# A gated mix of linear attention and a SwiGLU block: the order and the queues of the first loads, and the place of one group of gate matmuls

## The chip, the cores and the metric

The kernel runs on one core of a Trainium2 chip. The core has five engines with an instruction stream each: TensorE (PE, matrix multiply; PEld is its weight load), VectorE (DVE), ScalarE (ACT), GpSimd (POOL) and SyncE (SP). DMA transfers are issued by an engine's queue, here by SP and ScalarE, and are carried out by 16 DMA engines that all queues share. The metric is device time in microseconds (us) of one execution, as a median over runs; less is better.

## The reference, cut to what matters

`x` is 2048 tokens of 512 numbers in bf16. One weight per column gives each token a gate `g`; the result mixes a linear-attention block (32 heads of 16) and a SwiGLU block (hidden width 1376).

```python
g = sigmoid((x * gate_w).sum(-1, keepdims=True))
# a: linear attention
q, k, v = split(x @ wqkv)                  # 32 heads, 16 wide
phi = lambda t: where(t > 0, t + 1, exp(t)) + 1e-6
kv  = einsum("bhsd,bhse->bhde", phi(k), v) # a sum over all tokens
z   = einsum("bhsd->bhd", phi(k))
o   = einsum("bhqd,bhde->bhqe", phi(q), kv) / (einsum("bhqd,bhd->bhq", phi(q), z) + 1e-6)
a   = o @ wo
# b: SwiGLU
b   = (silu(x @ w1) * (x @ w3)) @ w2
out = g * a + (1 - g) * b
```

## The kernel before

The tokens are cut into 16 tiles of 128 (numbered 0 to 15) and 4 blocks of 4 tiles (0 to 3). A matmul contracts over the 128 partitions, so the 512 columns of `x` are 4 chunks (`KC`). `x` is needed in two layouts: as it lies in memory (`x_sb`) and transposed (`xT`, columns on the partitions). The transposed one comes from DMA loads that transpose on the way, except for tile 0, which TensorE transposes itself (`emit_xT`, lines 180 to 192: four transposes, one copy by VectorE, one by ScalarE, line 192).

All loads are issued at the start. SP's queue issues, in this order: tile 0 of `x` (line 83), the transposing load of tile 1 and one of tiles 2 and 3 together (lines 88 and 89), then for blocks 1, 2 and 3 a transposing load (line 92) and a plain load of some tiles of `x` (line 97), and then the weights: wq, the last 96 columns of w1 and w3, the gate weights (line 102: one two-byte number per partition and chunk), wv, w1, w3, wo, w2. ScalarE's queue issues only the k weights `wk` in two halves (lines 84 and 85), ahead of a small exponential that loads its table.

TensorE's order is written out by hand (`manual_schedule`); that of the other engines is the framework's, which also places all semaphores and waits. TensorE's stages are:

1. warm-up matmuls on constants (`emit_warm`, lines 163 to 176): five groups of four matmuls with 32 weight columns each, and one of 128 columns; the transposes of tile 0; three more warm-up matmuls (line 417);
2. the k matmuls of tiles 0 to 3 (lines 418 to 421; line 195), 4 for each tile, in the order of the tiles. Each tile's result goes through `phi`: an exponential on ScalarE (line 145), two instructions on VectorE (lines 147 and 150), and a sum on GpSimd;
3. the k matmuls of tiles 4 to 15, mixed with `x`-transposed times phi(k) (`XP`, line 215), which sums over all tokens;
4. the q matmuls of block 0 and the remainder columns with the gate column (`r_ps`, line 251), then `kv` (64 matmuls of 32 columns, line 467), whose product with a mask on VectorE (line 471) feeds the `W` matmuls (line 487). Between these stand the 16 matmuls of the first w1 chunk (`emit_gate_tiled`, lines 326 to 333), in groups of four, one group per chunk of the contraction;
5. the SwiGLU matmuls (lines 345 and 353) and the output matmuls (lines 386 to 395) of all blocks.

The loads have no inputs that the program makes, so the engine that issues them waits only where the framework has it wait; an engine's instructions go out in order, a DMA issue among them.

Of the kernel before, what the change touches and what calls it, by code (L numbers as in the profile page):

```python
# [11 lines left out]
ENG = mybir.EngineType  # L12
# [5 lines left out]
def kernel(  # L18
# [12 lines left out]
    nc = tc.nc  # L31
    P = nc.NUM_PARTITIONS
# [5 lines left out]
    KC = D // P  # L38
    NT = S // P
    TB = 512  # L40
# [3 lines left out]
    FR = F - FC * P  # L44
    FM = FC * P
    NR = 2 * FR + 1
# [5 lines left out]
    x2d = A_x.flatten_outer_dims()  # L52
# [13 lines left out]
    xT = consts.tile([P, KC, S], BF16, name="xT")  # L66
# [5 lines left out]
    wr_sb = consts.tile([P, KC, 2 * P], BF16, name="wr_sb")  # L72
# [7 lines left out]
    x_r = x2d.rearrange("(t p) d -> p t d", p=P)  # L80
    dq = nc.sync
    TF = 1
    dq.dma_start(out=x_sb[:, 0, :], in_=x2d[0:P, :])
    nc.scalar.dma_start(out=wk_sb[:, 0:2, :], in_=wqkv_r[:, 0:2, D : 2 * D])  # L84
    nc.scalar.dma_start(out=wk_sb[:, 2:4, :], in_=wqkv_r[:, 2:4, D : 2 * D])
    pre = consts.tile([1, 1], FP32, name="pre")
    nc.scalar.activation(out=pre[:], in_=nc.const_aps.tensor(0.0, [1, 1], FP32), func=ACT.Exp)
    for tsl in (slice(P, 2 * P), slice(2 * P, TB)):
        dq.dma_start(out=xT[:, :, tsl], in_=x2d[tsl, :], transpose=True)
    x_cut = [TF, TPB + 2, 3 * TPB, NT]  # L90
    for tb in range(1, NTB):
        dq.dma_start(
            out=xT[:, :, tb * TB : (tb + 1) * TB], in_=x2d[tb * TB : (tb + 1) * TB, :],
            transpose=True,
# [3 lines left out]
    dq.dma_start(out=wq_sb[:], in_=wqkv_r[:, :, 0:D])  # L98
    dq.dma_start(out=wr_sb[:, :, 0:FR], in_=w1_r[:, :, FM:F])
    dq.dma_start(out=wr_sb[:, :, FR : 2 * FR], in_=w3_r[:, :, FM:F])  # L100
    with nc.allow_non_contiguous_dma(reason="one gate weight per partition and chunk"):
        dq.dma_start(
            out=wr_sb[:, :, 2 * FR : NR], in_=gate_w.rearrange("(kc d o) -> d kc o", d=P, o=1)
        )
    dq.dma_start(out=wv_sb[:], in_=wqkv_r[:, :, 2 * D : 3 * D])
    dq.dma_start(out=w1_sb[:], in_=w1_r[:, :, 0:FM])
    for fsl in (slice(0, FM // 2), slice(FM // 2, FM)):
# [12 lines left out]
        out=bm, in_=bm, pattern=[[-Dh, HPC], [0, Dh]], compare_op=ALU.is_ge, fill=0.0,  # L120
# [3 lines left out]
        out=bm, in_=bm, pattern=[[Dh, HPC], [0, Dh]], compare_op=ALU.is_ge, fill=0.0,  # L124
# [38 lines left out]
    def emit_warm(tiled, whole, tag="XP3"):  # L163
        warm = psX.tile([P, TB], FP32, tag=tag, name="warm")
        for n in tiled:
            for i in range(NG):
                gsl = slice(i * G, (i + 1) * G)
                nc.tensor.matmul(
                    warm[gsl, 0:n], lhsT=warm_l[:, gsl], rhs=warm_r[:, 0:n], start=True, stop=True
                )  # L170
        for n in whole:
            nc.tensor.matmul(
                warm[:, 0:n], lhsT=warm_l, rhs=warm_r[:, 0:n], start=True, stop=True
            )

    emit_warm((TB, TB, TB, TB, TB), (P,))

    st = {}

    def emit_xT(t):  # L180
        for h in range(2):
            xTp = psX.tile([P, 2, P], BF16, tag=f"XP{(2 * t + h) % 4}", name="xTp")
            for j in range(2):
                kc = 2 * h + j
                nc.tensor.transpose(
                    out=xTp[:, j, :], in_=x_sb[:, t, kc * P : (kc + 1) * P], identity=ident[:]
                )
            xT_t = xT[:, 2 * h : 2 * h + 2, t * P : (t + 1) * P]
            if h == 0:
                nc.vector.tensor_copy(out=xT_t, in_=xTp[:])  # L190
            else:
                nc.scalar.activation(out=xT_t, in_=xTp[:], func=ACT.Copy)
# [27 lines left out]
    def emit_q(tb, tt, pool, tag):  # L220
        t = tb * TPB + tt
        ts_tok = slice(t * P, (t + 1) * P)
        if tt == 0:
            st[tb, "pq"] = blk.tile([P, TPB, D], BF16, tag="pq", name="pq")
            st[tb, "den"] = blk.tile([P, TPB, H], FP32, tag="den", name="den")
        q_ps = pool.tile([P, D], FP32, tag=tag, name="q_ps")
        for kc in range(KC):
            nc.tensor.matmul(  # L228
                q_ps[:], lhsT=xT[:, kc, ts_tok], rhs=wq_sb[:, kc, :],
                start=(kc == 0), stop=(kc == KC - 1),  # L230
            )
        phi(st[tb, "pq"][:, tt, :], q_ps[:])
# [54 lines left out]
    def emit_omg(tb):  # L287
        om = work.tile([P, TPB], FP32, tag="om", name="om")
        nc.vector.tensor_scalar(
            out=om[:], in0=st[tb, "el"][:], scalar1=2.0, scalar2=2.0, op0=ALU.mult,  # L290
            op1=ALU.add,
        )
        nc.vector.reciprocal(out=omg[:, tb * TPB : (tb + 1) * TPB], in_=om[:])
# [29 lines left out]
            )  # L323
        st[tb, "pqT"] = pqT

    def emit_gate_tiled(gate_ps):
        for kc in range(KC):
            for i in range(NG):
                gsl = slice(i * G, (i + 1) * G)
                nc.tensor.matmul(  # L330
                    gate_ps[gsl, :], lhsT=w1_sb[:, kc, gsl], rhs=xT[:, kc, 0:TB],
                    start=(kc == 0), stop=(kc == KC - 1),
                )
# [79 lines left out]


    k0 = [psM.tile([P, D], FP32, tag="mm", name=f"k0_{t}") for t in range(TPB)]
    emit_xT(0)
    emit_warm((), (P, P, P))
    for t in range(TPB):
        for kc in range(KC):
# [14 lines left out]
    with tc.manual_schedule(engines={ENG.DVE}):  # L434
        Q = 32
        NB = D // Q
        zt = consts.tile([P, NB, Q], FP32, name="zt")
        nc.vector.transpose(out=zt[:].rearrange("p b f -> p (b f)"), in_=pks[:])
        w = Q // 2
        while w >= 1:  # L440
            nc.gpsimd.tensor_add(zt[:, :, 0:w], zt[:, :, 0:w], zt[:, :, w : 2 * w])
            w //= 2
        zq = zt[:, :, 0]
        z_up = consts.tile([P // 2, NB], FP32, name="z_up")
        z_h = consts.tile([P // 2, NB], FP32, name="z_h")
        z_hi = consts.tile([Q, NB], FP32, name="z_hi")
        z_col = consts.tile([P, NB], FP32, name="z_col")
        nc.gpsimd.tensor_copy(z_up[:], zq[P // 2 : P, :])
        nc.gpsimd.tensor_add(z_h[:], zq[0 : P // 2, :], z_up[:])
        nc.gpsimd.tensor_copy(z_hi[:], z_h[Q : 2 * Q, :])  # L450
        for b in range(P // Q):
            nc.gpsimd.tensor_add(z_col[b * Q : (b + 1) * Q, :], z_h[0:Q, :], z_hi[:])
        for dc in range(KC):
            if dc % 2 == 0:
                nc.scalar.activation(out=XP_sb[:, dc, :], in_=XP_ps[dc][:], func=ACT.Copy)
            else:
                nc.vector.tensor_copy(out=XP_sb[:, dc, :], in_=XP_ps[dc][:])

        emit_q(0, TPB - 1, psM, "mm")
        rem0 = [emit_rem_mm(0, half, psM, "mm") for half in range(2)]  # L460
        kvT_ps = psX.tile([P, KC, G], FP32, tag="XP0", name="kvT_ps")
        gate0 = psM.tile([P, TB], FP32, tag="mm", name="gate0")
        for c in range(KC):
            for dc in range(KC):
                for i in range(NG):
                    bsl = slice(c * P + i * G, c * P + (i + 1) * G)
                    nc.tensor.matmul(  # L467
                        kvT_ps[i * G : (i + 1) * G, c, :], lhsT=wv_sb[:, dc, bsl],
                        rhs=XP_sb[:, dc, bsl], start=(dc == 0), stop=(dc == KC - 1),
                    )  # L470
        nc.vector.tensor_tensor(
            out=kvT_sb[:], in0=kvT_ps[:],
            in1=diagmask[:, None, :].to_broadcast([P, KC, G]), op=ALU.mult,
        )
        for half in range(2):
            emit_rem_h(0, half, *rem0[half])
        nc.vector.transpose(
            out=z_sb[:].rearrange("p (b f) -> p b f", f=Q),
            in_=z_col[:, :, None].to_broadcast([P, NB, Q]),
        )  # L480

        emit_gate_tiled(gate0)
        W_ps = [psX.tile([P, D], FP32, tag=f"XP{i}", name=f"W_ps{i}") for i in range(NG)]
        for i in range(NG):
            gsl = slice(i * G, (i + 1) * G)
            for c in range(KC):
                nc.tensor.matmul(  # L487
                    W_ps[i][c * G : (c + 1) * G, :], lhsT=kvT_sb[gsl, c, :],
                    rhs=wo_sb[gsl, c, :], start=True, stop=True,
                )  # L490

        emit_omg(0)
        emit_ffn(0, 0, gate=gate0)
# [72 lines left out]
```

## Time and profile before

| | us |
|---|---|
| median of 3 runs (178.19 to 178.46) | 178.42 |
| the profiled execution | 178.12 |
| its span, first to last instruction | 176.3 |
| TensorE matmuls busy | 172.7 |
| VectorE busy | 119.9 |
| GpSimd busy | 66.9 |
| ScalarE busy | 64.5 |

The profile is one execution. Its lines give start and length in us, the engine, the line of the kernel, the operation, output and inputs, the number of instructions merged and, in brackets, the idle time of the engine before them with what ended it. Of the DMA engines' work, the plain picture is a full load in the first third of the span and little after it:

```
DMA  5999999911002311124000101240002022300002
GB/s 174 236 271 281 262 386 363 348 45 26 9 4 60 67 37 37 37 63 89 0 0 7 58 20 47 59 82 0 6 7 67 7 66 54 66 4 0 30 30 60
```

Each digit is the busy share, in tenths, of a fortieth of the span.

### The profile page before, as it was taken

What the parts mean: (1) busy time and instruction counts of PE and PEld (TensorE: products, weight loads), DVE (VectorE), ACT (ScalarE), POOL (GpSimd) and SP (SyncE); (2) the same over time, 40 slices, a digit from 0 to 9 for tenths busy, and PEclk for the clock granted to TensorE, in tenths of its full rate; (3) what the DMA queues carried; (4) which work ended last, traced back from release to release, by engine and by line L of the source; (5) the groups of instructions that cost most, each with busy time, mean ns of one, the idle gap of its engine ahead of it and who ended that gap; (6) DMA issues with size and microseconds to landing.
All of it is one profiled execution on the core that took longest, in us unless ns stands there. A gap on an engine that the chain in (4) does not pass through costs nothing.

```text
span 176.3 us, 2655 instructions
## 1 busy us (share of the span) xinstructions
PE 172.7 (98%) x966; PEld 82.6 (47%) x966; DVE 119.9 (68%) x204; ACT 64.5 (37%) x121; POOL 66.9 (38%) x100
## 2 busy tenths in 40 slices
PE   8999999999999999999999999999999999999994
PEld 3344444464445454444454544444545444444463
DVE  0588778898999637597875466977854669776000
ACT  4442224475424333324243333233434323331222
POOL 7298555779109423282003232820032329100000
DMA  5999999911002311124000101240002022300002
GB/s 174 236 271 281 262 386 363 348 45 26 9 4 60 67 37 37 37 63 89 0 0 7 58 20 47 59 82 0 6 7 67 7 66 54 66 4 0 30 30 60
DMA packets 30524, 15.27 MB, mean 87 GB/s; under 512 B 21456, under 2 KB 30000, under 8 KB 30512
## 3 DMA queue, kind: packets, MB, share of 16 engines
q1 hardware_dynamic: 29824, 14.54, 30.3%
q10 hardware_dynamic: 688, 0.57, 1.0%
q8 instruction: 7, 0.11, 0.3%
q14 instruction: 5, 0.04, 0.1%
HBM read 8.42 MB, written 2.10 MB: 60 GB/s over the span
## 4 chain that ended last, share of the span: by engine, by line
PE 96%; DMA 2%; ACTq 0%; DVE 0%; issue 0%
PE up_ps L353 20%; PE o_ps L395 20%; PE gate_ps L345 19%; PE o_ps L386 8%; PE q_ps L228 8%; PE XP L215 8%; PE k_ps L195 6%; PE r_ps L251 3%; DMA wk_sb<-in_A_wqkv_dram 2%; PE o_ps L390 2%; PE k L195 2%; PE gate L330 0%; PE kvT_ps L467 0%; ACTq L84 0%; PE W_ps L487 0%; DVE o_last L404 0%
## 5 line engine op out<-in xcount | busy, mean ns | idle before, releaser
L353 PE MATMUL up_ps<-xT,w_sb 128*128 128x512 bf16 x160 | 41.1, 379 | 0.0
L345 PE MATMUL gate_ps<-xT,w_sb 128*128 128x512 bf16 x156 | 40.0, 379 | 0.0
L236 POOL TENSOR_TENSOR qz<-pq,z_sb 128x512 f32<-128x512 bf16 x16 | 18.5, 1164 | 53.5 <-DVE pq L150 53.5
L358 ACT ACTIVATE th<-gate_ps 128x512 bf16<-128x512 f32 x39 | 23.3, 597 | 39.8 <-PE gate_ps L345 38.3
L395 PE MATMUL o_ps<-w_sb,hT 128*128 128x512 bf16 (+3 forms) x180 | 37.5, 355 | 0.0
L360 DVE SCALAR_TENSOR_TENSOR gs<-th,gate_ps 128x512 bf16<-128x512 bf16 x39 | 26.6, 683 | 5.6 <-ACT th L358 5.3
L365 DVE TENSOR_TENSOR hT<-up_ps,gs 128x512 bf16<-128x512 f32 x40 | 27.5, 690 | 3.7 <-PE gate_ps L345 0.5
L147 DVE TENSOR_SCALAR phi_m<-phi_e 128x512 bf16<-128x512 bf16 x32 | 16.2, 507 | 19.6 <-ACT phi_e L145 19.5
L311 POOL TENSOR_TENSOR pqn<-pq,rden 128x256 bf16<-128x256 bf16 x32 | 19.0, 625 | 16.5 <-DVE rden L302 15.1
L395 PEld LDWEIGHTS <-hT 128*128 128x128 bf16 x180 | 16.9, 98 | 17.8
L353 PEld LDWEIGHTS <-w_sb 128*128 128x128 bf16 x160 | 15.6, 98 | 18.9 <-issue 0.2
L345 PEld LDWEIGHTS <-w_sb 128*128 128x128 bf16 x156 | 15.3, 98 | 18.4
L400 ACT ACTIVATE o_out<-o_ps,omg 128x512 bf16<-128x512 f32 x15 | 10.3, 687 | 28.7 <-PE o_ps L395 28.7
L205 POOL TENSOR_TENSOR pks<-pks,pk_sb 128x512 f32<-128x512 f32 x15 | 17.4, 1158 | 8.1 <-DVE pk_sb L150 7.6
L386 PE MATMUL o_ps<-W_sb,pqT 128*128 128x512 bf16 (+3 forms) x72 | 16.8, 355 | 0.0
L228 PE MATMUL q_ps<-wq_sb,xT 128*128 128x512 bf16 x64 | 16.4, 379 | 0.0
L239 DVE TENSOR_REDUCE den<-qz 128x32 f32<-128x512 f32 x16 | 11.0, 685 | 7.9 <-POOL qz L236 7.8
L215 PE MATMUL XP<-pk_sb,x_sb 128*128 128x512 bf16 x64 | 15.9, 379 | 0.0
L145 ACT ACTIVATE phi_e<-k_ps 128x512 bf16<-128x512 f32 x12 | 7.2, 597 | 14.4 <-PE k_ps L195 10.4
L145 ACT ACTIVATE phi_e<-q_ps 128x512 bf16<-128x512 f32 x16 | 9.6, 597 | 7.8 <-PE q_ps L228 7.8
L195 PE MATMUL k_ps<-wk_sb,xT 128*128 128x512 bf16 x48 | 12.0, 379 | 0.0
L150 DVE SCALAR_TENSOR_TENSOR pq<-q_ps,phi_m 128x512 bf16<-128x512 f32 x16 | 11.1, 691 | 0.5
(68 smaller groups left out, 119.4 us busy)
## 6 DMA issues: line engine op xcount, KB each, us to landing
w_sb<-in_B_w_dram SPq DMA_DIRECT2D x2, 1280.0 KB, 9.7
out_dram<-o_out SPq DMA_DIRECT2D x15, 128.0 KB, 1.7
w_sb<-in_B_w_dram SPq DMA_DIRECT2D x2, 640.0 KB, 8.3
x_sb<-in_A_x_dram SPq DMA_DIRECT2D x1, 768.0 KB, 5.2
x_sb<-in_A_x_dram SPq DMA_DIRECT2D x1, 640.0 KB, 4.4
wk_sb<-in_A_wqkv_dram ACTq DMA_DIRECT2D x2, 256.0 KB, 3.3
x_sb<-in_A_x_dram SPq DMA_DIRECT2D x1, 512.0 KB, 4.8
wq_sb<-in_A_wqkv_dram SPq DMA_DIRECT2D x1, 512.0 KB, 5.7
```

The costliest lines, as they stand in the source:

```text
L195: nc.tensor.matmul(k_ps[:], lhsT=xT[:, kc, t * P : (t + 1) * P], rhs=wk_sb[:, kc, :], start=(kc == 0), stop=(kc == KC - 1),)
L215: nc.tensor.matmul(XP_ps[dc][:], lhsT=x_sb[:, t, dc * P : (dc + 1) * P], rhs=pk_sb[:, t, :], start=(t == 0), stop=(t == NT - 1),)
L228: nc.tensor.matmul(q_ps[:], lhsT=xT[:, kc, ts_tok], rhs=wq_sb[:, kc, :], start=(kc == 0), stop=(kc == KC - 1),)
L236: nc.gpsimd.tensor_tensor(out=qz[:], in0=st[tb, "pq"][:, tt, :], in1=z_sb[:], op=ALU.mult)
L311: nc.gpsimd.tensor_tensor(out=pqn[:].rearrange("p (i c e) -> p c i e", i=NG, c=KC)[:, :, :, dsl], in0=st[tb, "pq"][:, tt, :].rearrange("p ...
L345: nc.tensor.matmul(gate_ps[:], lhsT=w1_sb[:, kc, fsl], rhs=xT[:, kc, tok_sl], start=(kc == 0), stop=(kc == KC - 1),)
L353: nc.tensor.matmul(up_ps[:], lhsT=w3_sb[:, kc, fsl], rhs=xT[:, kc, tok_sl], start=(kc == 0), stop=(kc == KC - 1),)
L358: nc.scalar.activation(out=th[:], in_=gate_ps[:], func=ACT.Tanh, scale=0.5)
L360: nc.vector.scalar_tensor_tensor(out=gs[:], in0=th[:], scalar=1.0, in1=gate_ps[:], op0=ALU.add, op1=ALU.mult)
L365: nc.vector.tensor_tensor(out=st[tb, "hT"][:, fc, :], in0=up_ps[:], in1=gs[:], op=ALU.mult)
L386: nc.tensor.matmul(o_ps[:], lhsT=st[tb, "pqT"][:, c, tsl], rhs=W_sb[:, c, a:b], start=(c == 0), stop=False,)
L395: nc.tensor.matmul(o_ps[:], lhsT=st[tb, "hT"][:, fc, tsl], rhs=w2_sb[:, fc, a:b], start=False, stop=(fc == FC - 1),)
```

## The change

Four edits. The gate weights are loaded in two halves; the first half is issued on SP's queue between tile 0 and tile 1, the second where the whole was. Of the load of tiles 2 and 3, tile 2 stays on SP's queue as a load of its own; tile 3 is loaded by ScalarE's queue, with ScalarE's order fixed by hand so that the load stands behind the copy of line 192. The one 128-column warm-up matmul ahead of the transposes goes. Of the 16 matmuls of the first w1 chunk, the first group of four moves into the middle of the `kv` matmuls.

```diff
+    gate_r = gate_w.rearrange("(kc d o) -> d kc o", d=P, o=1)
     dq.dma_start(out=x_sb[:, 0, :], in_=x2d[0:P, :])
     nc.scalar.dma_start(out=wk_sb[:, 0:2, :], in_=wqkv_r[:, 0:2, D : 2 * D])
     nc.scalar.dma_start(out=wk_sb[:, 2:4, :], in_=wqkv_r[:, 2:4, D : 2 * D])
...
-    for tsl in (slice(P, 2 * P), slice(2 * P, TB)):
+    def load_gate(ksl):
+        with nc.allow_non_contiguous_dma(reason="one gate weight per partition and chunk"):
+            dq.dma_start(out=wr_sb[:, ksl, 2 * FR : NR], in_=gate_r[:, ksl, :])
+
+    load_gate(slice(0, KC // 2))
+    for tsl in (slice(P, 2 * P), slice(2 * P, 3 * P)):
         dq.dma_start(out=xT[:, :, tsl], in_=x2d[tsl, :], transpose=True)
...
-    with nc.allow_non_contiguous_dma(reason="one gate weight per partition and chunk"):
-        dq.dma_start(
-            out=wr_sb[:, :, 2 * FR : NR], in_=gate_w.rearrange("(kc d o) -> d kc o", d=P, o=1)
-        )
+    load_gate(slice(KC // 2, KC))
...
-    emit_warm((TB, TB, TB, TB, TB), (P,))
+    emit_warm((TB, TB, TB, TB, TB), ())
...
-    def emit_gate_tiled(gate_ps):
-        for kc in range(KC):
+    def emit_gate_tiled(gate_ps, lo, hi):
+        for kc in range(lo, hi):
...
-    emit_xT(0)
+    with tc.manual_schedule(engines={ENG.Activation}):
+        emit_xT(0)
+        t3sl = slice(3 * P, TB)
+        nc.scalar.dma_start(out=xT[:, :, t3sl], in_=x2d[t3sl, :], transpose=True)
     emit_warm((), (P, P, P))
...
         for c in range(KC):
+            if c == KC // 2:
+                emit_gate_tiled(gate0, 0, 1)
             for dc in range(KC):
...
-        emit_gate_tiled(gate0)
+        emit_gate_tiled(gate0, 1, KC)
```

## The prediction

> **What bounds the kernel now.** First the top of the page, then the chain of waits, then the first 16 us in order of time, since all edits but one lie there.
>
> ```profile
> span 176.3 us, 2655 instructions
> ...
> PE 172.7 (98%) x966; PEld 82.6 (47%) x966; DVE 119.9 (68%) x204; ACT 64.5 (37%) x121; POOL 66.9 (38%) x100
> ```
>
> TensorE is busy for 172.7 of 176.3 us. Time is gained only in the 3.6 us in which it idles or where its clock is low, and a stall put in is absorbed by nothing behind it. The chain of waits begins so (start, length, what):
>
> ```profile
> 1.29 3.70 DMA wk_sb<-in_A_wqkv_dram
> 4.99 0.04 issue
> 5.03 3.34 PE k L195 x14
> 8.38 0.86 PE XP L215 x4
> ```
>
> The second half of wk (issued by ScalarE at 1.29) lands at 4.99; from there TensorE is never more than 0.2 us without work. The first k matmuls, in the order of time:
>
> ```profile
> 0.84 2.33 PE L168 MATMUL warm<-const-bfloat16-1.0 128*32 128x512 bf16 x20 [0.84 <-PEq L550]
> 1.26 2.62 SPq L89 DMA_TRANSPOSE xT<-in_A_x_dram  x2
> 3.85 0.38 ACT L192 ACTIVATE xT<-xTp 128x256 bf16<-128x256 bf16 x1 [0.54 <-PE xTp L185]
> 3.93 2.17 SPq L92 DMA_TRANSPOSE xT<-in_A_x_dram  x1
> 5.41 0.59 PEld L195 LDWEIGHTS <-xT 128*128 128x128 bf16 x4 [0.28 <-DMA xT<-in_A_x_dram]
> 5.66 0.60 ACT L145 ACTIVATE phi_e<-k 128x512 bf16<-128x512 f32 x1 [1.43 <-PE k L195]
> 6.47 1.41 PEld L195 LDWEIGHTS <-xT 128*128 128x128 bf16 x8 [0.48 <-DMA xT<-in_A_x_dram]
> 6.77 3.53 SPq L92 DMA_TRANSPOSE xT<-in_A_x_dram  x1
> 10.97 4.46 SPq L92 DMA_TRANSPOSE xT<-in_A_x_dram  x1
> ```
>
> Tile 1 arrives at 5.37 and is used at 5.41; tiles 2 and 3, one load, arrive at 6.4 and are used at 6.47. Tile 3's own first matmul starts at 7.35 in a finer window of this view. So each load comes just in time, with no slack. Landing times of the loads of lines 89 and 92, and the kinds of transposing loads:
>
> ```profile
> DMA to landing us min/median/max: 3.8/4.0/4.1
> DMA to landing us min/median/max: 4.3/5.7/8.0
> hTr<-hr SPq DMA_TRANSPOSE x16, 2.3
> pqT<-pqn SPq DMA_TRANSPOSE x16, 2.4
> xT<-in_A_x_dram SPq DMA_TRANSPOSE x5, 4.3
> ```
>
> By windows around single issues, 4.3, 5.7 and 8.0 belong to token blocks 1, 2 and 3 in this order. **All 37 transposing loads of the trace go out on SP's queue, none on ScalarE's.** The change makes the first that does not.
>
> **The parts, costed.**
>
> *Half the gate weights ahead of tile 1.* One more DMA issue on SP: 0.51 us by line 102, and a gap of 0.05. All that SP issues later moves by 0.55: tile 1 to 1.82 (until 3.10, at the 1.28 of line 89), tile 2 to 3.15, block 1 from 3.93 to 4.48, the x load to 6.69, block 2 from 6.77 to 7.31, block 3 from 10.97 to 11.5. The weights behind have room: wo lands at 22.75 + 9.9 = 32.7 and is first read at 38.74, w1 at 27.5 for 37.75. Cost by itself 0, hidden by that room; for tile 1, which has none, 0 to 0.55, bounded from below by a gain: while SP's queue holds back its transposing data, wk has the DMA engines to itself, and TensorE's wait for it (the second matmul starts at 4.24, the third at 5.03, against 0.22 to 0.43 in a run) could shrink by up to 0.5. I take -0.1.
>
> *Tile 2 alone.* Line 89's issues last 1.278 and 1.292 us for 128 and 256 tokens, so the smaller load saves SP nothing; it may land some 0.5 earlier (128 KB at the 250 GB/s of those slices). Counted with the first.
>
> *One warm-up matmul less.* 0.29 us at 3.10, where TensorE awaits x (0.81 + 2.2 = 3.03). Gain at most 0.1, but the next matmuls wait for wk until 5.03 anyway: 0. If the clock rose later for it, up to 0.2 lost.
>
> *A gate group inside kv.* The same 16 matmuls, 4 of them earlier:
>
> ```profile
> 37.27 0.66 PE L467 MATMUL kvT_ps<-XP_sb,wv_sb 128*32 128x32 bf16 x64
> 37.75 1.06 PE L330 MATMUL gate<-xT,w_sb 128*32 128x512 bf16 x16
> 38.02 0.29 DVE L471 TENSOR_TENSOR kvT_sb<-kvT_ps,diagmask 128x128 bf16<-128x128 f32 x1
> 38.74 0.43 PE L487 MATMUL W_ps<-wo_sb,kvT_sb 32*32 32x512 bf16 x16
> ```
>
> kv ends 0.22 later (a group of four takes 0.88 / 4), VectorE's product at about 38.5 instead of 38.31, and the W matmuls at 38.74 still find it. Cost 0, hidden by the three groups left; 0.2 without that cover.
>
> *Tile 3 on ScalarE's queue.* What ScalarE issues there it issues in order: behind the new load stand the exponentials of line 145, first at 5.66, and behind these VectorE's pk and all that reads it. Without a wait the load goes out at 4.24 (end of the copy) until 5.52, so the exponentials lose nothing, and it lands 2.4 to 4.1 later (rows of pqT and line 89): 6.7 to 8.3, for 7.35. With a wait the cost is large. The trace shows no pair of queues transposing at once, so the price is bounded from both sides: below by no wait, above by a wait for everything that SP loads transposed, up to block 3 (11.5 + 8.0 = 19.5). I assume that the framework, which writes all semaphores here, keeps transposing loads of two queues apart, and that the order in which it lists the instructions says who waits for whom. In the compiled program before (its list is not part of the profile) SP's loads through block 2 stand ahead of ScalarE's copy, block 3's behind it. So I take: tile 3 waits until block 2 has landed, and block 3 waits for tile 3.
>
> [...]
>
> The sum of this case: block 2 lands at 7.31 + 5.7 = 13.0, less some of the 0.5 for tile 3's data no longer ahead: 12.8. ScalarE issues at 12.85. Landing between 2.4 (quiet) and 4.1; only one x load is still in flight, so 3.0: 15.85, matmul at 15.9. Against 7.35 that is 8.55 lost. Meanwhile ScalarE is held until 14.1; three exponentials of 0.6 follow and are done by 15.9, so nothing is late for it. Block 3, at 15.9 + 8.0, is early for its k matmuls (near 23 before, now 33), and the weights move by 4.4, within their room. Then the clock: the warm-up groups of four stand 0.42 apart (20 in 2.33), the gate's 0.22, so TensorE starts at half rate, until at least 4.24, 3.4 us after its start. If 8 us of idling send it back there, 3.4 us at half rate cost 1.7; bounds 0 and 2.1 (half rate until 5.03). I take 1.7, since the start is the only row of TensorE after a rest.
>
> [...]
>
> Sum: 8.55 + 1.7 - 0.1 = 10.15. The profiled execution took 178.12 (span 176.3 and 1.8 around), so 188.3; the median of the runs, 178.42, lies 0.3 above it: **188.6**, with 186.5 to 190.5 for this case.
>
> **Rivals.**
>
> *Tile 3 waits for all of SP's transposing loads.* They stand ahead of it in the source, so a framework that goes by the source's order does this. Block 3 lands at 19.0 to 19.5 and the weights then fill the DMA engines, so tile 3 takes 4.1: 23.4, 16.05 late; with 1.7: 195.9, in the runs 196.2. Against it: the compiled order.
>
> *It waits for less.* For block 1: 4.48 + 4.3 = 8.8, landing 11.8 to 12.9, 4.5 to 5.6 late, with up to 1.7 of clock. For tile 2 alone (6.0): tile 3 lands 8.5 to 10.1, block 1 waits for it and lands 4.3 later at 12.8 to 14.4, for 9.2. Both give some 182 to 186; I put 184.5. For it: at 4.24 the trace has SP in the middle of block 1's issue.
>
> *No wait at all: faster.* Place: the wait for wk until 5.03. If both queues transpose at once and tile 3 lands by 7.35, wk up to 0.5 earlier and tile 1 no later than 5.2 bring the whole k stage forward by 0.5 at most; 0.25 on the way there: 177.9, range 177.6 to 179.0. It decides from tile 1's landing: below 5.4 it gains, at 5.9 it loses 0.5. For it: every load here meets its matmul within 0.1, so small moves count. Against it: the assumption on the framework.
>
> **How the numbers follow.** Block 2: 0.42; all: 0.30; less: 0.13; no wait: 0.15. The predicted time is the first's. The range 181.5 to 198 leaves out the last case and little at the ends, some 0.18. A measurement here tells about 0.2% (0.36 us) from no change; of the no-wait case 0.10 is faster by more, 0.03 within, 0.02 slower; with the rest slower 0.87.
>
> **What would show it.** A transposing issue on ScalarE's queue with a long wait ahead of it and the first exponential late; weight loads of tile 3's k matmuls waiting for xT, by 8 us (block 2), 16 (all), 1 to 5 (less) or about nothing; the issue time of block 3 on SP (moved behind tile 3 in the first case, near 11.5 in the second); matmuls behind the stall 0.43 apart, not 0.22. The prediction is wrong if ScalarE's load goes out near 4.3, or if its wait ends with another load.

## The result, and the profile after

The change makes the kernel slower by 6.6%:

| | us |
|---|---|
| before, median of 6 runs (178.19 to 179.05) | 178.45 |
| after, median of 6 runs (189.09 to 191.43) | 190.06 |
| ratio after to before, 95% interval | 1.066 (1.063 to 1.070) |
| span of the profiled execution, before and after | 176.3 and 188.2 |

First the top of the page of the changed kernel, with the busy share of TensorE and its granted clock in 40 slices of the span:

```profile
span 188.2 us, 2642 instructions
...
PE 173.8 (92%) x949; PEld 82.9 (44%) x965; DVE 117.9 (63%) x204; ACT 64.1 (34%) x121; POOL 66.8 (35%) x100
...
PE   7702999999999999999999999999999999999994
...
PEclk9995899999999999999999999999999999999999
```

TensorE is busy 1.1 us longer than before (172.7 there), in a span 11.9 us longer: most of the time is idle time, and it lies in the first four slices. In the fourth the clock is down to half (5 in the row of PEclk). The chain of waits says what TensorE waits for there (start, length, what):

```profile
7.27 6.71 DMA xT<-in_A_x_dram
13.98 0.02 issue
14.00 3.65 DMA xT<-in_A_x_dram
17.64 0.05 issue
17.69 1.89 PE k L198 x4
```

Two transposing loads stand one behind the other. The first is block 2's, issued by SP at 7.27 and landed at 13.98; the second is tile 3's on ScalarE's queue. The engines' own lines, in the order of time:

```profile
3.99 0.38 ACT L195 ACTIVATE xT<-xTp 128x256 bf16<-128x256 bf16 x1 [0.68 <-PE xTp L188]
7.27 4.68 SPq L98 DMA_TRANSPOSE xT<-in_A_x_dram  x1
14.00 1.27 ACTq L422 DMA_TRANSPOSE xT<-in_A_x_dram  x1
15.32 1.58 ACT L148 ACTIVATE phi_e<-k 128x512 bf16<-128x512 f32 x3 [10.95 <-issue]
17.66 2.05 SPq L98 DMA_TRANSPOSE xT<-in_A_x_dram  x1
17.69 1.89 PE k L198 x4
```

ScalarE has its copy done at 4.37, then does nothing until 14.00, 0.02 us after block 2 has landed; the exponentials of tiles 0 to 2, the first of which came at 5.66 before, stand behind the load and come at 15.32. SP's next transposing load, block 3's, goes out at 17.66, 0.02 after tile 3 has landed. So each queue waits for the other's transposing loads. Tile 3's k matmuls start at 17.69 instead of 7.35, as this line of the kernel before has it:

```profile
7.35 1.03 PE L195 MATMUL k<-wk_sb,xT 128*128 128x512 bf16 x4
```

Of the gate group inside kv (TensorE and VectorE in the order of time):

```profile
49.01 0.38 PE L475 MATMUL kvT_ps<-XP_sb,wv_sb 128*32 128x32 bf16 x32
49.22 0.41 PE L333 MATMUL gate<-xT,w_sb 128*32 128x512 bf16 x4
49.44 0.41 PE L475 MATMUL kvT_ps<-XP_sb,wv_sb 128*32 128x32 bf16 x32
49.67 0.84 PE L333 MATMUL gate<-xT,w_sb 128*32 128x512 bf16 x12
49.94 0.29 DVE L479 TENSOR_TENSOR kvT_sb<-kvT_ps,diagmask 128x128 bf16<-128x128 f32 x1 [0.40 <-PE kvT_ps L475]
50.44 0.43 PE L495 MATMUL W_ps<-wo_sb,kvT_sb 32*32 32x512 bf16 x16
```

VectorE's product now waits 0.40 for kv and ends at 50.23, while the three gate groups left occupy TensorE until the W matmuls at 50.44.

### The profile page after: what moved, and what is told of

It reads as the page before. It is cut to its first block, busy times and chain, and to the rows that moved or that the text cites. A ratio compares the mean times of both kernels' runs of the same rounds, so it can differ in the third digit from the quotient of the medians.

```text
span 188.2 us, 2642 instructions
## 1 busy us (share of the span) xinstructions
PE 173.8 (92%) x949; PEld 82.9 (44%) x965; DVE 117.9 (63%) x204; ACT 64.1 (34%) x121; POOL 66.8 (35%) x100
## 4 chain that ended last, share of the span: by engine, by line
PE 89%; DMA 6%; SPq 3%; issue 1%; DVE 0%
PE up_ps L356 18%; PE o_ps L398 18%; PE gate_ps L348 18%; PE XP L218 7%; PE o_ps L389 7%; PE q_ps L231 7%; DMA xT<-in_A_x_dram 6%; PE k_ps L198 5%; PE r_ps L254 3%; PE o_ps L393 2%; SPq L95 1%; SPq L98 1%; PE k L198 1%; PE gate L333 0%; SPq L103 0%
## 5 line engine op out<-in xcount | busy, mean ns | idle before, releaser
L150 DVE TENSOR_SCALAR phi_m<-phi_e 128x512 bf16<-128x512 bf16 x32 | 14.1, 441 | 33.0 <-ACT phi_e L148 33.0
L198 PE MATMUL k<-wk_sb,xT 128*128 128x512 bf16 x16 | 5.8, 512 | 9.6 <-DMA xT<-in_A_x_dram 9.1
L198 PEld LDWEIGHTS <-xT 128*128 128x128 bf16 x64 | 6.3, 102 | 18.8 <-DMA xT<-in_A_x_dram 10.1
```

The lines of the kernel that those rows point to most:

```text
L198: nc.tensor.matmul(k_ps[:], lhsT=xT[:, kc, t * P : (t + 1) * P], rhs=wk_sb[:, kc, :], start=(kc == 0), stop=(kc == KC - 1),)
```

## The experiments

All times are medians beside runs of the kernel before on the same chip; the ratio is to these, with its 95% interval.

**One part alone: tile 3's load.**

```diff
 # on the kernel before
-    for tsl in (slice(P, 2 * P), slice(2 * P, TB)):
+    for tsl in (slice(P, 2 * P), slice(2 * P, 3 * P)):
...
-    emit_xT(0)
+    with tc.manual_schedule(engines={ENG.Activation}):
+        emit_xT(0)
+        t3sl = slice(3 * P, TB)
+        nc.scalar.dma_start(out=xT[:, :, t3sl], in_=x2d[t3sl, :], transpose=True)
```

> The kernel before with one part of the change alone: tile 3's transposing load on ScalarE's queue behind the copy, tile 2 alone on SP's; no early gate weights, the warm-up matmul and the gate group as before. Theory (the wait for block 2 is the whole of the loss): about 189.5, 11 us above before, ScalarE's load issued when block 2 has landed (near 13), a stall of some 10 us at tile 3's k matmuls and block 3's load issued behind tile 3. Rival (the early gate weights, which delay x, wk and all of SP's queue, carry a good part of it): 185 or less.

Measured: 189.9 against 178.38, 1.065 (1.062 to 1.069). This part is the whole loss. Its chain has the same two loads:

```profile
6.70 5.91 DMA xT<-in_A_x_dram
...
12.70 3.28 DMA xT<-in_A_x_dram
15.98 0.05 issue
16.03 1.89 PE k L195 x4
```

Yet the stall in this profile is 1.7 us shorter than in the changed kernel's (16.03 against 17.69 for tile 3's first matmul), at the same median time. That is taken up below, with the clock.

**All but that part.**

```diff
 # on the changed kernel
-    for tsl in (slice(P, 2 * P), slice(2 * P, 3 * P)):
+    for tsl in (slice(P, 2 * P), slice(2 * P, TB)):
...
-    with tc.manual_schedule(engines={ENG.Activation}):
-        emit_xT(0)
-        t3sl = slice(3 * P, TB)
-        nc.scalar.dma_start(out=xT[:, :, t3sl], in_=x2d[t3sl, :], transpose=True)
+    emit_xT(0)
```

> The changed kernel with tiles 2 and 3 again in one load on SP's queue; the early half of the gate weights, the missing warm-up matmul and the gate group inside kv stay. Theory (these three are small): 178.4 to 179.4. By the changed kernel's trace wk lands 0.7 us later with the gate weights ahead, so rather 179 than 178.4. Rival (they lose several us that the stall hides): 181 or more. Rival (they gain): under 178.1.

Measured: 178.99, 1.005 (1.002 to 1.007): the other edits together lose 0.4 to 1.3 us.

**The order decides what is waited for.** In the compiled program (its list is not part of the profile) SP's loads through block 2 stood ahead of tile 3's. Two kernels move this border, by an edge in the order of the instructions; the loads themselves and their order on SP stay.

```diff
 # on the changed kernel; the loads of lines 96 to 115 now follow tile 3's in the source
-        nc.scalar.dma_start(out=xT[:, :, t3sl], in_=x2d[t3sl, :], transpose=True)
+        t3_ins = nc.scalar.dma_start(out=xT[:, :, t3sl], in_=x2d[t3sl, :], transpose=True)
+    def behind(**kw):
+        ins = nc.sync.dma_start(**kw)
+        tc.add_manual_dep(
+            ins.ins, t3_ins.ins.name,
+            mybir.DependencyInfo(mybir.DependencyClass.NoSync, mybir.DependencyReason.DATA),
+            reason="behind tile 3",
+        )
...
+    for tb in range(1, NTB):
+        issue = behind if tb > 1 else dq.dma_start   # block 1 ahead; else: behind for all
```

> The changed kernel with all of SP's loads behind tile 2 (block 1 and on) put behind ScalarE's load of tile 3 in the order of the instructions. Theory (ScalarE's load waits for whichever transposing loads SP has ahead of it in that order, and the next one of SP's waits for it): ScalarE issues when tile 2 has landed, near 6.5, tile 3 lands at 9 to 10.5, block 1 some 4.3 later; loss 3.5 to 7, so 182 to 185.5. Rival (the cost is in ScalarE's queue itself, whatever stands ahead): 188 or more. Rival (the source's order counts, in which nothing was ahead here but tiles 1 and 2): the same as the theory, so this run speaks only against a fixed cost.

> The same with block 1's two loads left ahead of tile 3 and all others behind it. Theory: ScalarE issues when block 1 has landed (near 9), tile 3 lands at 12 to 13, k matmuls of tile 3 about 5 us late, clock loss 0 to 1.7: 183.5 to 185.5. With the changed kernel this gives three steps of one wait: tile 2, block 1, block 2. Rival (a fixed cost): 188 or more.

| ahead of tile 3 on SP | ScalarE issues | tile 3's first matmul | time | ratio |
|---|---|---|---|---|
| tile 2 | 6.59 | 9.32 | 184.65 | 1.034 (1.032 to 1.036) |
| block 1 | 9.00 | 12.37 | 184.83 | 1.036 (1.034 to 1.039) |
| block 2 (the change) | 14.00 | 17.69 | 190.06 | 1.066 (1.063 to 1.070) |

ScalarE's load goes out when the last one ahead of it has landed (6.51, 8.91 and 13.98 by the chains), three times over, and there is no fixed cost near 188. The first two end at the same time for different reasons, as the chain with only tile 2 ahead shows:

```profile
3.06 3.45 DMA xT<-in_A_x_dram
...
6.59 2.68 DMA xT<-in_A_x_dram
9.27 0.02 issue
9.29 4.17 DMA xT<-in_A_x_dram
13.46 0.05 issue
13.50 4.45 PE k_ps L177 x12
```

Tile 3 is only 2.0 late here, but block 1 now waits for tile 3: it goes out at 9.29, not 3.93, and its matmuls start at 13.50 against 9.24 before:

```profile
9.24 2.59 PE k_ps L195 x12
```

So the wait between the two queues is paid on both sides here: tile 3 is 2.0 late, block 1's matmuls 4.3.

**The same place and queue, but no transposing.**

```diff
 # on the changed kernel
-        nc.scalar.dma_start(out=xT[:, :, t3sl], in_=x2d[t3sl, :], transpose=True)
+        nc.scalar.dma_start(out=x_sb[:, 3, :], in_=x2d[3 * P : TB, :])
...
     for t in range(TPB):
+        if t == TPB - 1:
+            emit_xT(t)
         for kc in range(KC):
             emit_k_mm(k0[t], t, kc)
```

> The changed kernel with tile 3 loaded plain by ScalarE's queue at the same place (behind its first copy) and transposed by TensorE, as tile 0 is; block 1's plain load of x is cut around tile 3. So the queue, the place and the time of issue stay, and the transposing load from a second queue goes. Theory (the wait is there because both queues transpose): no wait, ScalarE's load goes out near 4.4, 178.8 to 179.8 (four transposes 0.3, their copies up to 0.6, late wk 0.5). Rival (any load at this place waits, or is late): 185 or more.

Block 1's plain load of `x` is cut in two around tile 3 as well. Measured: 181.38, 1.020 (1.016 to 1.024), between the two. The wait for block 2 is gone, but the load is late all the same:

```profile
1.30 4.28 DMA wk_sb<-in_A_wqkv_dram
5.58 0.02 issue
5.60 3.93 DMA x_sb<-in_A_x_dram
9.53 0.05 issue
9.57 0.30 PE xTp L188 x2
```

It goes out at 5.60, 0.02 after wk's second half has landed, though it needs nothing of wk; why it waits there isn't shown. It then takes 3.93 us to land, not the 2.5 of tile 0 in this profile (2.2 before), and the transposes and their copies hold tile 3's first matmul until 10.25. So 8.7 of the changed kernel's 11.6 us (8.3 by the ratios) go with the transposing from a second queue, and a load first issued at this place misses 7.35 even without it. A version that transposes on both queues without the wait wasn't tried.

**The clock.** 40 warm-up matmuls between the k matmuls of tiles 2 and 3 keep TensorE at work in the stall of the changed kernel; the wait stays.

```diff
 # on the changed kernel
     for t in range(TPB):
+        if t == TPB - 1:
+            emit_warm((), (TB,) * 40, tag="XP2")
         for kc in range(KC):
```

> The changed kernel with 40 warm-up matmuls of 512 columns (8.6 us at full rate) on constants between the k matmuls of tiles 2 and 3, so that TensorE does not rest in the stall; the wait stays. Theory (of the 11.6 us some 10.3 are the wait and 1.3 to 1.7 the clock after the rest): 188.4 to 188.8, k matmuls behind the stall 0.22 us apart. Rival (the rest beyond the wait has another cause, such as late weights): no change from 190.

Measured: 189.31, 1.060 (1.057 to 1.063): 1.2 us less than the changed kernel by the ratios (0.0066 of 178.4). That is 0.5 above the expected band, between it and the rival's 190, and the two kernels' intervals just touch; the profiled execution, the fastest of the four, took 188.43. Its stall is nearly the same (tile 3's first matmul at 17.41 after 17.69), and its mean granted clock is 0.998 after 0.981, so what was saved there is the clock. The windows of the changed kernel (from:to, length, busy time and count of PE, PEld, DVE, ACT and POOL, granted clock, DMA share, GB/s):

```profile
12.00:13.60 1.60, 0.00 (x0) 0.00 (x0) 0.00 (x0) 0.00 (x0) 0.00 (x0) 1.00 1.27 268
13.60:17.60 4.00, 0.00 (x0) 0.00 (x0) 1.58 (x4) 1.58 (x3) 0.56 (x1) 0.51 0.75 212
17.60:20.40 2.80, 2.71 (x7) 1.04 (x8) 1.35 (x4) 0.60 (x1) 2.31 (x3) 0.50 0.55 115
20.40:22.40 2.00, 1.95 (x10) 0.86 (x9) 0.88 (x2) 0.52 (x1) 0.98 (x2) 0.97 0.90 224
```

and of the kernel with tile 3's part alone:

```profile
12.00:16.00 4.00, 0.00 (x0) 0.00 (x0) 1.28 (x4) 1.57 (x3) 0.26 (x1) 0.50 0.76 221
16.00:21.00 5.00, 4.97 (x12) 1.79 (x13) 2.88 (x5) 0.60 (x1) 3.50 (x4) 0.50 0.75 185
21.00:23.00 2.00, 2.00 (x10) 0.88 (x9) 1.05 (x3) 1.19 (x2) 0.31 (x1) 0.99 1.05 337
```

At half clock TensorE works for 2.8 us in the first and 5.0 us in the second, which loses 1.4 and 2.5. With the stalls of 10.34 and 8.68 that makes 11.7 and 11.2, for spans 11.9 and 11.3 longer than before. So in these two executions the clock took back 1.1 of the 1.7 us by which the stall was shorter. These lengths belong to the executions, not to the kernels: the mean granted clock is 0.973, some 10.2 us at half clock, in four of the changed kernel's six executions and in three of the four with tile 3's part alone, and 0.98, some 7 us, in the others. If the clock nevertheless took more from the kernel with tile 3's part alone, the fill must save more there:

```diff
 # on the kernel with tile 3's part alone
     for t in range(TPB):
+        if t == TPB - 1:
+            emit_warm((), (TB,) * 38, tag="XP2")
```

> Tile 3's load alone on ScalarE's queue, as in the run of that part alone, with 38 warm-up matmuls of 512 columns (8.2 us at full rate) in the stall. There the stall was 8.7 us against 10.3 of the changed kernel, yet the times were the same, 189.9 and 190.06. Theory (the half clock ate the difference: it covered 5.0 us of matmuls there, 2.8 in the changed kernel, which costs 2.5 and 1.4): with the clock kept up, the wait alone is left, 178.4 + 8.7 to 9.3 = 187.1 to 187.7, some 2 us under the run without the fill, where the changed kernel gained about 1.2 by it. Rival (another loss makes the two equal): 188.7 or more.

Measured: 187.91, 1.053 (1.049 to 1.057): 2.2 us less than without the fill (0.0125 of 178.4), as expected. With the clock at 0.998 to 1.000 in every run of both filled kernels, their ratios differ by 0.0068, 1.2 us, and their intervals lie just apart: there the shorter wait does show. But each of the two savings, 2.2 and 1.2, is uncertain by about 0.8 us, so that the second is the larger is indicated, not shown. The time itself is 0.2 above the stated band; in its profile block 2 took 6.75 us to land, not 5.91, and the stall was longer by it.

**The early gate weights.**

```diff
 # on the kernel before; load_gate as in the change
+    load_gate(slice(0, KC // 2))
     for tsl in (slice(P, 2 * P), slice(2 * P, TB)):
...
+    load_gate(slice(KC // 2, KC))   # in place of the load of line 102
```

> The kernel before with the first half of the gate weights issued ahead of tile 1, nothing else. My prediction took -0.1 us for it (wk alone on the DMA engines while SP's queue holds back). The changed kernel's trace speaks against it: wk landed at 5.65 there, 4.99 before. If the small gate packets hold up wk: 178.9 to 179.3, with the third k matmul near 5.7. If the prediction's term holds: 178.3, the third k matmul at 5.0 or earlier.

Measured: 178.96, 1.0026 (1.0000 to 1.0052), with wk later than before (4.99):

```profile
1.30 4.27 DMA wk_sb<-in_A_wqkv_dram
5.57 0.04 issue
5.61 3.35 PE k L199 x14
```

Is it the number of two-byte pieces, or that something stands ahead of tile 1? With all of the gate weights there:

> The kernel before with all the gate weights (512 two-byte pieces) ahead of tile 1, not half of them. If the pieces themselves hold up wk, twice as many hold it up twice as long: wk near 6.1 against 5.6 with half and 5.0 without, 179.2 to 179.7. If it is the issue ahead, whatever it carries: as with half, 178.9.

Measured: 178.71, 1.0029 (1.0009 to 1.0049); wk lands at 5.43. Twice the pieces cost no more than half of them. And with wk's second half in that place instead:

```diff
 # on the kernel before
-    nc.scalar.dma_start(out=wk_sb[:, 2:4, :], in_=wqkv_r[:, 2:4, D : 2 * D])
+    dq.dma_start(out=wk_sb[:, 2:4, :], in_=wqkv_r[:, 2:4, D : 2 * D])
```

> The kernel before with the second half of wk issued on SP's queue between tile 0 and tile 1, in place of ScalarE's queue: tile 1's load is held back by one issue (0.5 us), as by the early gate weights, but by a load of 1 KB pieces that TensorE waits for. Theory (in the early-gate runs wk came 0.6 later because of the two-byte pieces, not because the transposing loads were held back): wk lands at 5.0 or earlier, tile 1 near 5.5, 177.9 to 178.5. Rival (holding the transposing loads back is itself what costs): the k stage 0.5 later, 178.9.

Measured: 178.48, 1.0003 (0.9989 to 1.0016). wk lands at 4.7 (issued 1.26, 3.4 to landing), but tile 1 arrives at 5.85, not near 5.5, and TensorE waits for that:

```profile
1.73 4.12 DMA xT<-in_A_x_dram
5.85 0.05 issue
```

So a load ahead of tile 1 does not by itself hold up wk, and nothing is gained, because tile 1 is needed next. wk's landing differs between executions too: it lies at 4.7 to 5.3 in the five profiles without early gate weights and at 5.4 to 5.9 in the eight with them. That the gate weights delay wk is thus shown, by how much is not; and why the small load does it, whatever its size, stays open.

**The gate group inside kv alone.**

```diff
 # on the kernel before; emit_gate_tiled with its bounds as in the change
+            if c == KC // 2:
+                emit_gate_tiled(gate0, 0, 1)
...
-        emit_gate_tiled(gate0)
+        emit_gate_tiled(gate0, 1, KC)
```

> The kernel before with the first group of gate matmuls inside kv, nothing else. Prediction: hidden, 178.3 to 178.6. Rival (VectorE's product of kv comes 0.2 later and the W matmuls with it): 178.65 or more.

Measured: 178.72, 1.0011 (0.9997 to 1.0025). The median lies in the rival's band (178.65 or more), but the interval holds no change. The stage itself says it is hidden: from the first remainder matmul to the first up matmul it takes 3.19 us,

```profile
36.64 1.33 PE r_ps L251 x16
39.83 0.97 PE up_ps L353 x4
```

and 3.17 before:

```profile
36.00 1.33 PE r_ps L251 x16
39.17 0.97 PE up_ps L353 x4
```

The 0.64 by which this execution is later lies ahead of the stage; wk landed at 5.26 there, against 4.99. The missing warm-up matmul wasn't tried alone.

No version here beats the kernel before; wk on SP's queue and the gate group inside kv are level with it.

## Why the prediction was right

The case forecast, its direction and its place are the measured ones: tile 3 waits for block 2, block 3 for tile 3, the exponentials stand behind the load, and the matmuls behind the stall run at half rate (tile 3's four in 1.89 us at a granted clock of 0.50, 1.03 before). The kernel with tile 3's part alone shows that nothing else carries the loss. Forecast 188.6, measured 190.06, inside the case's own 186.5 to 190.5. By its terms:

| term of the sum | forecast | measured |
|---|---|---|
| block 2 lands | 12.8 | 13.98 |
| tile 3's load, issue to landing | 3.0 | 3.65 |
| tile 3's first k matmul later by | 8.55 | 10.34 |
| the clock | 1.7 | 1.2 (fill), 1.4 (trace) |
| the early gate weights | -0.1 | hidden here; alone 1.0026 (1.0000 to 1.0052) |
| sum | 10.15 | 11.6 |

The terms that were mis-sized are the two landings. Block 2 was priced by its 5.7 of the trace before, less a part of 0.5 for data no longer ahead of it; it took 6.7 here and 5.9 to 6.8 in the runs with tile 3's part alone. Tile 3 lay between the stated bounds of 2.4 and 4.1, nearer to 4.1 than was taken.

The clock's term came near partly by luck. That a rest of 8 us brings one stretch of 3.4 us at half rate behind the stall was the author's estimate from TensorE's start in the trace of before; no run shows it after a rest of that length. In the profile of the changed kernel, after a rest of 9.1 us, it was 6.8 us, begun inside the stall, of which 2.8 us covered matmuls; with tile 3's part alone the clock cost 2.5 by the profile, above the stated bound of 2.1. (The second k matmul before, read there as starting at 4.24, starts at 4.39 by its own row.)

The rival by which tile 3 waits for all of SP's loads fell: block 3 was issued behind tile 3, not ahead of it. The one with a shorter wait was right as a price, 184.5 for what measured 184.65 and 184.83 when it was built on purpose. The one without a wait was wrong in a step: "the load goes out at 4.24". A plain load at that place went out at 5.60 and landed at 9.53, 2.2 past tile 3's need, so if a transposing load without the wait were as late, the case of 177.9 was too good by some 2 us.

The step on the early gate weights had the wrong sign: it said that "wk has the DMA engines to itself", but behind the gate weights wk came 0.4 to 0.7 later in the profiles of the change and of these two experiments than before it. The steps on kv and on the room of the weights held: no engine waited for a weight other than wk in the changed kernel though block 3 went out 6.7 us later.

## What to carry to other kernels

Before a transposing load moves to a second queue, list what the first queue has in flight in the order the framework compiled, not in the source: in these runs the load waited for the last of these (in the changed kernel until 14.00, block 2 having landed at 13.98), the first queue's next one waited for it (block 3 went out at 17.66), and what was queued behind it on its engine waited too (the first exponential came at 15.32, not 5.66). When a stall is inserted or removed, price the clock apart from the wait, and as a range: two profiled executions whose stalls differed by 1.7 us differed by 0.6 in their spans, because the half clock covered 5.0 us of matmuls in one and 2.8 in the other.

## What the runs showed of the hardware that was not expected

The clock was at half in stretches of about 3.4 us, or of two or three times that. In the changed kernel it was at half from 13.7 to 20.5, which is 6.8; with tile 3's part alone from 10.8 to 21.0, 10.2; in the two kernels with shorter waits from 14.0 to 17.4 and from 13.7 to 17.1, 3.4 each. What sets the length was not shown. It isn't the kernel alone: with only tile 2 ahead three executions have a mean granted clock of 0.991, which makes some 3.3 us at half clock, and the fourth, the fastest at 183.93, has 1.000, none; the changed kernel's six have some 7 us or some 10.

In the two kernels with shorter waits the longest rests ahead of the half clock were 2.3 us (11.22 to 13.50, one tile and one block late) and 2.0 us (10.41 to 12.37), and the clock fell 0.5 and 1.3 us after TensorE was at work again. In the changed kernel TensorE stopped at 8.58 and the clock fell 5.1 us later, with tile 3's part alone at 7.17 and 3.6 us later, both inside the stall. So no single time from the stop to the fall fits the four profiles: it was 2.8, 3.3, 5.1 and 3.6 us.

The granted clock in the profile's windows says 1.00 for the first microseconds before and after the change, though the warm-up groups there stand 0.42 apart, twice the 0.22 of the gate groups. The first entry of the changed kernel's clock records is the start of a full-clock stretch, at 6.88; the trace of before has no entry. With block 1 ahead the windows from 6 to 10 say 1.00 as well, and there ten k matmuls take 4.43, some 0.43 each, against 2.38 for the same ten with tile 3's part alone:

```profile
5.98 4.43 PE L177 MATMUL k<-wk_sb,xT 128*128 128x512 bf16 x10 [0.56 <-DMA wk_sb<-in_A_wqkv_dram]
```

So the state of the clock early in these runs has to be read from the matmuls.
